# Adding the further spectral products of a block convolution by accumulating DMAs on GpSimd's queue instead of VectorE, with all orders searched anew

## The chip, the cores and the metric

The kernel runs on one core of a Trainium2 chip. The metric is device time in microseconds (us), from one launch. Times are medians over runs. The profile is one profiled execution, in microseconds from the first instruction.

## The reference

Two blocks, each used twice, on x of 2048 tokens by 512 channels in bfloat16. Block A is a long convolution with a gate; block B is a SwiGLU feed-forward network of width 1792. Cut to what matters:

```python
def A(n, k, v, shift_k, ssm_k, ssm_D):          # n = layernorm(x)
    k_shift = sum(k_pad[:, t:t + S, :] * shift_k[:, 3 - t] for t in range(4))
    kv = k_shift * v
    y = irfft(rfft(kv, 2 * S) * rfft(ssm_k, 2 * S))[:S]   # causal, length 2048
    return n * (y + kv * ssm_D)

def B(n, w_gate, w_up, w_down):
    return (silu(n @ w_gate) * (n @ w_up)) @ w_down

x = q
for _ in range(2):
    x = x + A(layernorm(x), k, v, shift_k, ssm_k, ssm_D)
    x = x + B(layernorm(x), w_gate, w_up, w_down)
```

The convolved sequence y does not depend on x: k, v and the filter are inputs. It is computed once and used by both layers.

## The kernel before

**Blocks and spectra.** The sequence is cut into four blocks of 512 tokens. The causal convolution of length 2048 becomes a convolution of blocks: a block k of the result is the sum of the products of the spectrum X[i] of an input block with the spectrum G[j] of a filter block over i + j = k. A spectrum is a tile of 128 partitions by 4096 bfloat16 elements, which is 1 MB: four residue classes, real and imaginary part, 512 channels.

**A product.** `product(i, j)` (L740) multiplies X[i] by G[j]. Two multiplications of 128x4096 (L765) write the temporaries t1 and t2. Two combinations of 128x2048 (L769) form the real and the imaginary part. For the first product that belongs to a Z[k] they write Z[k] itself. For a further product they write over t1, and an addition of 128x4096 (L773) adds t1 to Z[k]. All of these are on VectorE (DVE). Six products are further ones: (1,0) into Z[1]; (0,2) and (2,0) into Z[2]; (2,1), (0,3) and (3,0) into Z[3].

**From Z to the result.** `inverse(k)` (L786) folds a full Z[k] on DVE: two rows of 128x2048 into a tile m (L653), then two sums and differences (L659) and two rotated ones (L670) of 128x1024 each back into Z. TensorE (PE) multiplies the four residue classes with an inverse matrix (L423, `ps<-Z,inv`), and ScalarE (ACT) copies them into Yk. The `prologue` of a unit (a layer, a block and a half block of 256 tokens) multiplies Yk by the normalised x (L998), adds x (L999), and computes layer statistics (L926). A power on GpSimd (POOL, L912) makes rstd of them, which L976 uses on DVE to normalise z. Two transposing DMAs on SyncE's queue (SP, L1006) bring z into zT, which the gate and up matmuls of the unit read (L423, `pf<-wg_sb,zT` and others). The feed-forward part goes on with an activation and a copy on ACT (L1197, L1198), a product on DVE (L1201, L1204), transposing DMAs on SP (L1206) and down matmuls (L1287); L1258, L1262 and L1267 are the same for units whose rows need no transposing.

**The order.** Each operation is recorded with `add(engine, cost, ...)` into a `Plan`. A table ORDER of 1798 numbers, one for each operation in the order of recording, sorts them; each engine then issues its own operations strictly in that sequence. `Plan.walk` goes once through the sequence with the recorded costs to place buffers into slots (spectra, t1, t2 and others share a ring of 11 slots, "s8") and to place filler matmuls. POOL carries 32 powers of L912 after the setup and no DMA.

Of the kernel before, what the change touches and what calls it, by code (L numbers as in the profile page):

```python
# [14 lines left out]
ALU = mybir.AluOpType  # L15
# [7 lines left out]
K_ACT = lambda b: b in {2, 3}  # L23
PW = 0.7
# [326 lines left out]
def kernel(  # L351
# [14 lines left out]
    nc = tc.nc  # L366
# [46 lines left out]
    add = plan.add  # L413
# [326 lines left out]
    def product(i, j, slots=range(4), conv=True):  # L740
# [31 lines left out]
        if not first:  # L772
            dve(8 * D, lambda: nc.vector.tensor_add(out=z.t[:], in0=z.t[:], in1=t1.t[:]), [t1], [z], conv=conv)  # L773
# [832 lines left out]
```

## Time and profile before

| what | value |
|---|---|
| time, median of 3 runs | 338.73 us (338.35 to 338.96) |
| span of the profiled execution | 337.1 us |
| what lies around the span (median less span; the profiled execution's own whole time is not listed apart from its span) | 1.6 us |
| mean granted TensorE clock | 1.000 |
| additions of L773, six | 13.7 us on DVE |
| DMA data moved | 31.08 MB, of which 30.61 MB on SP's queue |

A row of the profile's groups gives line, engine, operation, tiles out and in, shape, count, then the busy time in us and the mean time of one in ns, then the idle time of the engine just before such rows. PE is the matmul stream and PEld the loading of weights beside it. A table by windows gives the busy time of each engine in a stretch. The chain of waits follows the last instruction back through what released each step.

### The profile page before, as it was taken

How to read it: one execution, taken by the hardware profiler on the slowest of the kernel's cores; microseconds unless marked ns; L12 is line 12 of the kernel's file. 1: busy time of each engine (PE TensorE's matmuls, PEld its weight loads, DVE VectorE, ACT ScalarE, POOL GpSimd, SP SyncE). 2: the span in 40 equal slices, each digit the busy share in tenths (PEclk: the TensorE clock that was granted, in tenths of full speed). 3: DMA queues.
4: the chain of work that ended last, by engine and by line, in shares of the span. 5: the costliest groups of instructions: out<-in, count | busy, mean ns of one | idle time of the engine just before them, and what ended most of it. 6: DMA issues, size and time to landing. Idle time of an engine off the chain costs nothing.

```text
span 337.1 us, 6249 instructions
## 1 busy us (share of the span) xinstructions
PE 332.4 (99%) x2300; PEld 208.0 (62%) x2300; DVE 314.3 (93%) x566; ACT 269.4 (80%) x550; POOL 36.1 (11%) x48
## 2 busy tenths in 40 slices
PE   9999999999999999999999999999999999999996
PEld 7665865645445564644545474654445787878994
DVE  7799999999999999999999999997898998986995
ACT  6999999999966684989999794989765748476862
POOL 4010100031210100022110200021000000000000
PEclk9999999999999999999999999999999999999999
DMA  7999403632354446253314433320415320203001
GB/s 278 331 281 387 65 3 77 140 93 34 78 94 86 95 88 146 72 80 74 69 33 83 104 81 102 81 53 10 84 33 95 65 65 16 42 8 64 2 33 62
DMA packets 75817, 31.08 MB, mean 92 GB/s; under 512 B 67589, under 2 KB 73610, under 8 KB 75786
## 3 DMA queue, kind: packets, MB, share of 16 engines
q1 hardware_dynamic: 75632, 30.61, 38.3%
q8 instruction: 18, 0.29, 0.4%
q14 instruction: 13, 0.11, 0.1%
q10 hardware_dynamic: 154, 0.07, 0.1%
HBM read 12.33 MB, written 2.10 MB: 43 GB/s over the span
## 4 chain that ended last, share of the span: by engine, by line
PE 85%; DVE 10%; ACT 2%; issue 1%; POOL 0%; POOLq 0%
PE pf L423 48%; PE pd L1287 19%; PE ps L1097 7%; PE ps L423 6%; PE pf L1171 4%; DVE t L755 1%; PE wm L1572 1%; DVE Z L759 1%; DVE bst L926 1%; DVE t L769 1%; ACT jk L950 1%; DVE Z L773 1%; DVE t L765 1%; DVE m L896 1%; DVE z L976 1%
## 5 line engine op out<-in xcount | busy, mean ns | idle before, releaser
L423 PEld LDWEIGHTS <-zT 128*128 128x128 bf16 x496 | 48.5, 98 | 55.1 <-issue 0.2
L423 PE MATMUL pf<-wu_sb,zT 128*128 128x512 bf16 x248 | 61.5, 379 | 0.0
L423 PE MATMUL pf<-wg_sb,zT 128*128 128x512 bf16 x248 | 61.4, 379 | 0.0
L423 PE MATMUL pf<-zT,wg_sb 128*128 128x256 bf16 x400 | 50.7, 273 | 0.3 <-DVE zT L1037 0.3
L1197 ACT ACTIVATE sg<-pf 128x512 bf16<-128x512 f32 x62 | 37.4, 615 | 14.9 <-PE pf L423 10.7
L1287 PE MATMUL pd<-wd_sb,sg 128*128 128x512 bf16 x200 | 48.9, 379 | 0.0
L1198 ACT CAST hr<-pf 128x512 bf16<-128x512 f32 x62 | 36.3, 599 | 12.7 <-PE pf L423 10.9
L423 PEld LDWEIGHTS <-wg_sb 128*128 128x128 bf16 x400 | 38.6, 98 | 8.3 <-issue 0.7
L765 DVE TENSOR_TENSOR t<-X,G 128x4096 bf16<-128x4096 bf16 x18 | 41.0, 2287 | 0.1
L1258 ACT ACTIVATE sg<-pf 128x512 bf16<-128x512 f32 x50 | 29.6, 603 | 7.7 <-PE pf L423 6.3
L423 PE MATMUL pf<-zT,wu_sb 128*128 128x256 bf16 x272 | 34.9, 273 | 0.1
L912 POOL TENSOR_TENSOR rstd<-mv,nhalf 128x2 f32<-128x2 f32 x20 | 18.3, 919 | 147.8 <-DVE mv L927 147.8
L1287 PEld LDWEIGHTS <-sg 128*128 128x128 bf16 x200 | 19.6, 98 | 21.4
L423 PEld LDWEIGHTS <-wu_sb 128*128 128x128 bf16 x272 | 26.5, 98 | 6.6 <-issue 0.4
L1287 PE MATMUL pd<-wd_sb,ht 128*128 128x512 bf16 (+1 forms) x126 | 29.6, 369 | 0.0
L912 POOL TENSOR_TENSOR rstd<-ve,nhalf 128x2 f32<-128x2 f32 x12 | 13.8, 1150 | 119.6 <-ACT ve L954 119.6
L926 DVE BATCH_NORM_STATS2 bst<-xc 128x6 f32<-128x512 bf16 x40 | 26.3, 685 | 0.3
L1262 ACT CAST ht<-pf 128x512 bf16<-128x512 f32 x34 | 20.2, 599 | 1.6 <-PE pf L423 1.5
L1287 PEld LDWEIGHTS <-ht 128*128 128x128 bf16 x126 | 12.3, 98 | 13.4 <-DVE ht L1267 0.4
L532 ACT ACTIVATE X<-ps 128x512 bf16<-128x512 f32 x32 | 18.6, 606 | 2.3 <-PE ps L423 1.6
L1267 DVE TENSOR_TENSOR ht<-ht,sg 128x1024 bf16<-128x1024 bf16 (+1 forms) x33 | 18.3, 556 | 0.7 <-ACT sg L1258 0.4
L1204 DVE TENSOR_TENSOR hr<-hr,sg 128x1024 bf16<-128x1024 bf16 x25 | 17.1, 683 | 1.3 <-ACT sg L1197 0.9
(157 smaller groups left out, 590.9 us busy)
## 6 DMA issues: line engine op xcount, KB each, us to landing
hn<-in_A_ssm_k_dram SPq DMA_DIRECT2D x4, 512.0 KB, 4.0
vt<-in_A_v_dram SPq DMA_DIRECT2D x4, 512.0 KB, 6.0
xc<-in_A_q_dram SPq DMA_DIRECT2D x4, 512.0 KB, 5.3
out_dram<-xc SPq DMA_DIRECT2D x15, 128.0 KB, 1.9
wg_sb<-in_B_w_gate_dram SPq DMA_DIRECT2D x1, 1792.0 KB
wu_sb<-in_B_w_up_dram SPq DMA_DIRECT2D x1, 1792.0 KB, 7.6
wd_sb<-in_B_w_down_dram SPq DMA_DIRECT2D x1, 1280.0 KB, 11.5
sg<-hr SPq DMA_TRANSPOSE x62, 2.4
```

Source lines behind the costliest of these rows:

```text
L423: nc.tensor.matmul(o, lhsT=lhsT, rhs=rhs, start=(n == 0), stop=(n == len(terms) - 1))
L532: add("ACT", act(D), lambda: nc.scalar.activation(out=view(), in_=ps.t[:], func=ACT.Copy, scale=scale), r=[ps], w=[(buf, keys)], conv=conv)
L765: dve(8 * D, lambda t=t, part=part: nc.vector.tensor_mul(out=t.t[:], in0=x.t[:, :, part:part + 1, :].to_broadcast((P, R, 2, D)), in1=g.t[: ...
L912: add("POOL", cost, lambda: nc.gpsimd.tensor_tensor(out=rstd.t[:], in0=var(), in1=nhalf.t[:].to_broadcast((P, n)), op=ALU.pow), r=reads + ...
L926: add("DVE", 0.6, lambda st=st, i=i: nc.vector.bn_stats(out=st.t[:, 0:6], in_=xs[c].t[:, i, :]), r=[(xs[c], (i,))], w=[st])
L1097: nc.tensor.matmul(bank.t[:, half_ * C:(half_ + 1) * C], lhsT=lhsT(i), rhs=rhs(i), start=(first and i == 0 and half_ == 0), stop=(last and ...
L1197: add("ACT", act(D), lambda ps=ps, dst=dst, o=o, which=which: nc.scalar.activation(out=rows(dst, o), in_=ps.t[:], func=ACT.Silu) if which ...
L1198: out=rows(dst, o), in_=ps.t[:], func=ACT.Silu) if which == "g" else nc.scalar.copy(out=rows(dst, o), in_=ps.t[:]),
L1258: add("ACT", act(D), lambda ps=ps, o=o, sg=sg: nc.scalar.activation(out=sg.t[:, o:o + 2, :], in_=ps.t[:], func=ACT.Silu), r=[ps], w=[(sg, ...
L1262: add("ACT", act(D), lambda ps=ps, o=o, ht=ht: nc.scalar.copy(out=ht.t[:, o:o + 2, :], in_=ps.t[:]), r=[ps], w=[(ht, (o // 2,))], due=(uni ...
L1267: dve(n * W, lambda sg=sg, ht=ht: nc.vector.tensor_mul(out=ht.t[:], in0=ht.t[:], in1=sg.t[:]), [sg], [ht], due=(unit, k / pairs, 0.0, "h"))
L1287: nc.tensor.matmul((pds[o] if not cs.start else pds[HP]).t[:, cs], lhsT=ht.tiles(q, o), rhs=wt["d"].t[:, ft, cs], start=(ft == std0 and no ...
```

## The change

`Z_DMA` is true for every pair. In place of the DVE addition of a further product, `product` records an accumulating DMA on GpSimd's queue: it reads t1 and the old Z, and writes their sum into Z, SBUF to SBUF. The table ORDER is replaced as a whole: each operation of the kernel may stand elsewhere.

```diff
@@ -21,6 +21,7 @@
 K_ACT = lambda b: b in {2, 3}
+Z_DMA = lambda i, j: True
 PW = 0.7
...
 ORDER = [
-    13, 127, 133, 202, 6, 0, 2, 4, 21, 5, 8, 1, 3, 9, 11, 17, 12, 18, 14, 19, 22, 20, 25, 24, 23, 26, 27, 37, 28, 31, 38, 69, 36, 60, 16, 52, 44,
...
+    10, 5, 7, 203, 0, 3, 4, 8, 17, 1, 2, 35, 37, 38, 89, 6, 12, 9, 11, 13, 22, 15, 18, 14, 16, 19, 20, 32, 33, 91, 95, 96, 39, 46, 49, 50,
...
@@ -769,7 +773,9 @@
-        if not first:
+        if not first and Z_DMA(i, j):
+            add("POOL", 1.3, lambda: nc.gpsimd.dma_start(out=z.t[:], in_=t1.t[:], accum_op=ALU.add, max_dma_last_dim=4096), r=[t1], w=[z], lat=7.0, conv=conv)
+        elif not first:
             dve(8 * D, lambda: nc.vector.tensor_add(out=z.t[:], in0=z.t[:], in1=t1.t[:]), [t1], [z], conv=conv)
```

The numbers 1.3 and 7.0 are what the planner counts for the DMA on POOL and until it has landed; they steer the order and the slots only. The operations of PE are the same in number (2267 matmuls and 33 fillers), in another order. The six DMAs are called A1 to A6 below, in the order of issue: A1 adds (1,0) to Z[1], A2 and A3 add (0,2) and (2,0) to Z[2], and A4 to A6 add (2,1), (0,3) and (3,0) to Z[3].

What stands where is shown at three places. A row is line, operation, tile written and tiles read (each with the number of its buffer), shape, and in brackets the semaphores it waits for: DVE_49 is VectorE's own, DMASW that of a GpSimd DMA, DMAHW that of a DMA of another queue. The lines of the changed kernel lie 4 to 6 further on: L653, L765, L769, L773, L912, L976, L1201 and L1267 of before are L657, L769, L773, L777 (now the DMA), L918, L982, L1207 and L1273.

VectorE before, around the last further product, (3,0) into Z[3]. The two rows z are the normalising for the unit of layer 2, block 2 (blocks count from 0), second half, whose transposed form zT PE waits for:

```order
L765 TENSOR_TENSOR t2_3060<-X3_2818,G0_255 128x4096 [waits DVE_49]
L1201 TENSOR_TENSOR hr_3062<-hr_3062,sg_3026 128x512 [waits Activation_49]
L976 TENSOR_SCALAR z_3069<-xc_1859,nm_3041,rstd_3067 128x512 [waits Pool_49]
L976 TENSOR_SCALAR z_3079<-xc_1859,nm_3041,rstd_3067 128x512 [waits DMAHW6_49]
L765 TENSOR_TENSOR t1_3081<-X3_2818,G0_255 128x4096
L769 TENSOR_TENSOR t1_3081<-t1_3081,t2_3060 128x4x512 [waits DVE_49]
L769 TENSOR_TENSOR t1_3081<-t1_3081,t2_3060 128x4x512
L1201 TENSOR_TENSOR hr_3062<-hr_3062,sg_3026 128x512 [waits Activation_49]
L773 TENSOR_TENSOR Z_2286<-Z_2286,t1_3081 128x4096 [waits DVE_49]
L653 TENSOR_TENSOR m_3098<-Z_2286 128x2048 [waits DVE_49]
```

VectorE in the changed kernel, at the same product:

```order
L769 TENSOR_TENSOR t1_3013<-X3_2734,G0_237 128x4096
L1210 TENSOR_TENSOR hr_2939<-hr_2939,sg_2997 128x1024 [waits Activation_49]
L773 TENSOR_TENSOR t1_3013<-t1_3013,t2_2962 128x4x512 [waits DVE_49]
L773 TENSOR_TENSOR t1_3013<-t1_3013,t2_2962 128x4x512
L982 TENSOR_SCALAR z_3101<-xc_1837,nm_3020,rstd_3099 128x512 [waits Pool_49]
L982 TENSOR_SCALAR z_3112<-xc_1837,nm_3020,rstd_3099 128x512 [waits DMAHW6_49]
L1207 TENSOR_TENSOR hr_3047<-hr_3047,sg_3029 128x512 [waits Activation_49]
L982 TENSOR_SCALAR n_3135<-xc_2648,mv_2732,rstd_2790 128x512
L1273 TENSOR_TENSOR ht_3069<-ht_3069,sg_3088 128x512 [waits Activation_49]
L982 TENSOR_SCALAR n_3135<-xc_2648,mv_2732,rstd_2790 128x512
L1207 TENSOR_TENSOR hr_3047<-hr_3047,sg_3029 128x512
L657 TENSOR_TENSOR m_3163<-Z_2264 128x2048 [waits DMASW5_49]
```

The second multiplication and the two combinations stood behind the rows z and stand ahead of them now; the addition is gone, and the first fold of Z[3] (m) waits for DMASW5, which is A6, with seven short rows between.

GpSimd before, at the same place (rstd_3067 is the one that the rows z read):

```order
L912 TENSOR_TENSOR rstd_2900<-ve_2898,nhalf_122 128x2 [waits Activation_49,Pool_49]
L912 TENSOR_TENSOR rstd_2969<-ve_2960,nhalf_122 128x2 [waits Activation_49]
L912 TENSOR_TENSOR rstd_3065<-mv_2766,nhalf_122 128x2 [waits DVE_49,Pool_49]
L912 TENSOR_TENSOR rstd_3067<-ve_3058,nhalf_122 128x2 [waits Activation_49,Pool_49]
L912 TENSOR_TENSOR rstd_3231<-mv_3218,nhalf_122 128x2 [waits DVE_49,Pool_49]
L912 TENSOR_TENSOR rstd_3388<-mv_3374,nhalf_122 128x2 [waits DVE_49,Pool_49]
```

GpSimd in the changed kernel (rstd_3099 is the one that the rows z read now):

```order
L918 TENSOR_TENSOR rstd_2827<-mv_2823,nhalf_87 128x2 [waits DVE_49,Pool_49]
L918 TENSOR_TENSOR rstd_2960<-ve_2958,nhalf_87 128x2 [waits Activation_49,Pool_49]
L918 TENSOR_TENSOR rstd_3099<-ve_3033,nhalf_87 128x2 [waits Activation_49,Pool_49]
L777 DMA Z_2264<-t1_3013 128x2x2048 [waits DMASW4_49,DVE_49]
L918 TENSOR_TENSOR rstd_3231<-mv_3228,nhalf_87 128x2 [waits DVE_49,Pool_49]
L918 TENSOR_TENSOR rstd_3440<-mv_3322,nhalf_87 128x2 [waits DVE_49,Pool_49]
```

A6 is queued right behind the power for the rows z, and the power of a later unit right behind A6.

VectorE before, at (0,2) into Z[2]; m and X2 are the folding of the input spectrum X[2], and t2_1792 belongs to the next product, (2,0):

```order
L769 TENSOR_TENSOR t1_1653<-t1_1653,t2_1650 128x4x512
L1267 TENSOR_TENSOR ht_1691<-ht_1691,sg_1738 128x1024 [waits DMAHW0_49,DMAHW5_49,PE_49,Activation_49]
L653 TENSOR_TENSOR m_1772<-X2_1492 128x2048 [waits DMAHW4_49,DMAHW3_49,DMAHW1_49]
L653 TENSOR_TENSOR m_1772<-X2_1492 128x2048
L659 TENSOR_TENSOR X2_1492<-m_1772 128x1024 [waits DVE_49]
L670 TENSOR_TENSOR X2_1492<-m_1772 128x2x512
L1267 TENSOR_TENSOR ht_1644<-ht_1644,sg_1779 128x512 [waits Activation_49]
L659 TENSOR_TENSOR X2_1492<-m_1772 128x1024
L670 TENSOR_TENSOR X2_1492<-m_1772 128x2x512
L765 TENSOR_TENSOR t2_1792<-X2_1492,G0_255 128x4096 [waits DVE_49]
L773 TENSOR_TENSOR Z_1614<-Z_1614,t1_1653 128x4096
```

VectorE in the changed kernel, at the same product:

```order
L773 TENSOR_TENSOR t1_1647<-t1_1647,t2_1642 128x4x512
L1345 TENSOR_TENSOR xc_301<-xc_301,dn_1684 128x1024 [waits Activation_49]
L657 TENSOR_TENSOR m_1733<-X2_1471 128x2048 [waits DVE_49]
L657 TENSOR_TENSOR m_1733<-X2_1471 128x2048
L674 TENSOR_TENSOR X2_1471<-m_1733 128x2x512 [waits DVE_49]
L1273 TENSOR_TENSOR ht_1703<-ht_1703,sg_1771 128x1024 [waits DMAHW6_49,DMAHW5_49,Activation_49]
L1273 TENSOR_TENSOR ht_1758<-ht_1758,sg_1769 128x512 [waits PE_49]
L663 TENSOR_TENSOR X2_1471<-m_1733 128x1024
L674 TENSOR_TENSOR X2_1471<-m_1733 128x2x512
L663 TENSOR_TENSOR X2_1471<-m_1733 128x1024
L769 TENSOR_TENSOR t1_1797<-X2_1471,G0_237 128x4096 [waits DVE_49]
L769 TENSOR_TENSOR t2_1799<-X2_1471,G0_237 128x4096 [waits DMASW1_49]
```

The addition at the end is gone. The second multiplication of the product (2,0) stands behind its first one, and waits for DMASW1, which is A2, since t2_1799 takes the slot that A2 reads from.

141 rows, old and new, of the table ORDER are left out of this document.

## Prediction

> **What bounds the kernel now.** I read the page's busy times first, then the windows, the waits of TensorE, the chain, and the timeline at the last product. The page, with busy time, share of the span and number of instructions:
>
> ```profile
> span 337.1 us, 6249 instructions
> PE 332.4 (99%) x2300; PEld 208.0 (62%) x2300; DVE 314.3 (93%) x566; ACT 269.4 (80%) x550; POOL 36.1 (11%) x48
> ```
>
> The span is 337.1 us and the median of the runs 338.73, so 1.6 us lie around the span. I take these 1.6 as unchanged: every term below is a difference in the span, and is put on 338.7. PE is busy 99% of it. The windows say where the rest is (length, then busy time of PE, PEld, DVE, ACT, POOL, the granted clock, the DMA share, GB/s):
>
> ```profile
> 0.00:33.00 33.00, 31.73 (x295) 21.76 (x295) 28.74 (x74) 29.03 (x59) 5.97 (x18) 1.00 1.00 319
> 33.00:60.00 27.00, 26.91 (x186) 18.23 (x187) 26.86 (x38) 26.86 (x60) 2.52 (x3) 1.00 0.32 54
> 160.00:210.00 50.00, 50.00 (x277) 26.94 (x276) 49.48 (x63) 41.66 (x80) 3.86 (x3) 1.00 0.35 79
> 235.00:262.00 27.00, 26.95 (x146) 13.86 (x145) 24.55 (x37) 18.16 (x37) 1.38 (x2) 1.00 0.36 69
> 300.00:334.00 34.00, 33.84 (x348) 29.32 (x346) 28.43 (x76) 23.08 (x47) 1.38 (x2) 1.00 0.13 29
> ```
>
> Ahead of 33 us PE idles 1.27 us (33.00 less 31.73), where no further product runs. In the three other windows with any idle time it is 0.09 + 0.05 + 0.16 = 0.30 us. DVE is nearly full (49.48 of 50), and PE does not wait for it. The waits of PE and its weight loads, largest of their kind (total, times, longest):
>
> ```profile
> PE ptz L1034 <- DVE z L976: 0.3, 1, 0.3
> PEld L1034 <- DVE z L976: 0.8, 1, 0.8
> PEld L423 <- DVE Z L659: 0.3, 1, 0.3
> PEld L423 <- DMA zT<-z: 0.2, 1, 0.2
> ```
>
> A weight load that waits costs PE only what its buffered matmuls do not cover, so these lines bound from above and the 0.30 us is the price. The bound is PE's own stream. A full DVE matters only where its work is just in time, and the chain goes over DVE at one of the six further products, (3,0) into Z[3] (start, length, step):
>
> ```profile
> 239.22 0.67 DVE z L976 x2
> 239.89 2.21 DVE t L765
> 242.12 2.36 DVE t L769 x2
> 244.82 2.21 DVE Z L773
> 248.62 1.15 DVE m L653
> 250.40 0.68 DVE Z L670
> ```
>
> **The change: what goes.** The groups concerned (count, then busy time and mean ns):
>
> ```profile
> L773 DVE TENSOR_TENSOR Z<-Z,t 128x4096 bf16<-128x4096 bf16 x6 | 13.7, 2287 | 0.0
> L765 DVE TENSOR_TENSOR t<-X,G 128x4096 bf16<-128x4096 bf16 x18 | 41.0, 2287 | 0.1
> L653 DVE TENSOR_TENSOR m<-Z 128x2048 bf16<-128x2048 bf16 x6 | 7.2, 1213 | 0.1
> L670 DVE TENSOR_TENSOR Z<-m 128x1024 bf16<-128x1024 bf16 x6 | 4.0, 680 | 0.0
> L976 DVE TENSOR_SCALAR z<-xc,nm,rstd 128x512 bf16<-128x512 bf16 x4 | 1.5, 408 | 0.0
> ```
>
> Six additions of 2.287 us leave DVE: 13.7 us of 314.3. Freed time on an engine for which PE hardly waits is worth at most PE's idle time, 0.30 us after 33 us. I take -0.3, with ends 0 and -0.3. The start has the same instructions in another order: 0, with ends of -1.27 (all idle time gone) and +1.3 (the same again).
>
> **What comes: the price of one accumulating DMA.** No row shows one. The nearest are plain loads (KB, median us to landing), and POOL's powers, which share the engine that issues it (min/median/max ns):
>
> ```profile
> hn<-in_A_ssm_k_dram SPq DMA_DIRECT2D x4, 512.0 KB, 4.0
> wu_sb<-in_B_w_up_dram SPq DMA_DIRECT2D x1, 1792.0 KB, 7.6
> L912 POOL TENSOR_TENSOR rstd<-mv,nhalf x20: 688/812/1503, 30.4 to 306.7; 128x2 f32<-128x2 f32 x20
> L912 POOL TENSOR_TENSOR rstd<-ve,nhalf x12: 687/750/2863, 17.2 to 238.4; 128x2 f32<-128x2 f32 x12
> ```
>
> From 512 to 1792 KB it is 3.6 us for 1.25 MB, 2.9 us a MB. One MB moved plainly comes to 4.0 + 1.4 = 5.4 us; counting the two MB that an addition reads, 8.3. I take the middle, 6.9, since reading and writing may overlap. POOL's share I bound by its shortest and longest power, 0.7 and 2.9, and take 1.1, near the medians. From issue to landing that makes 8.0 us, with ends of 6.1 and 11.2. POOL is 11% busy; behind a DMA in its queue stands a power at most, which a POOL held for 2.9 us would delay by that much.
>
> **Where the landing is waited for.** The order of the changed kernel gives the rows between the end of a product and the first row that needs its DMA. For A2 they are two folds (2.4), four rotations and sums (2.7), three rows xc and ht (1.8: two of L670's size, one of L976's) and a multiplication (2.3): 9.2 us. A1, A3 and A4 have 9 to 11 us by the same count, and A5 far more. At 8.0 none of these waits; at 11.2 A2 waits 2.0 and the others up to 2.2, each after a saving of 2.3 in the same queue. Behind the waiting t2 in A2's case are only DVE's products, which PE reads much later. I take 0 for A1 to A5.
>
> A6 has seven rows of about 0.41 us, 2.9 us, before the first fold of Z[3], so DVE will wait there with everything behind it: the fold, the products hr of the feed-forward part, then the prologue of block 3. What counts is when PE is late. The timeline of before there (start, length, engine, line; in brackets the idle time before it):
>
> ```profile
> 238.43 0.69 POOL L912 TENSOR_TENSOR rstd<-ve,nhalf 128x2 f32<-128x2 f32 x1 [6.19 <-ACT ve L954]
> 239.15 0.73 DVE L976 TENSOR_SCALAR z<-xc,nm,rstd 128x512 bf16<-128x512 bf16 x2
> 239.59 2.52 SPq L1006 DMA_TRANSPOSE zT<-z  x2
> 242.26 1.03 PE L423 MATMUL pf<-wg_sb,zT 128*128 128x512 bf16 x4
> 243.12 1.03 PE L423 MATMUL pf<-wu_sb,zT 128*128 128x512 bf16 x4
> 251.32 1.03 PE L423 MATMUL ps<-Z,inv 128*128 128x512 bf16 x4
> ```
>
> In the changed kernel the product ends ahead of the rows z, and A6 stands behind the same power in POOL, so it is issued at 239.1 (238.43 + 0.69). PE needs Z[3] two matmuls earlier than before, at 251.32 - 0.43 = 250.9 (four matmuls take 0.86 us, from 242.26 to 243.12). Two folds and one sum ahead of that are 2.4 + 0.7 = 3.1 us, and the hand-over 0.3 by the wait on L659 above. So A6 must land by 247.5, 8.4 us after its issue. At 8.0 it does, and the wait costs nothing; at 11.2 it is 2.8 us late, at 6.1 2.3 early. I take 0, with ends 0 and 2.8.
>
> By the Trainium skill, page "SBUF — State Buffer", section "Who interferes with whom", a DMA issued by GpSimd can starve for the writing of its descriptors while DVE runs an instruction in a two-port mode, which tensor_scalar can enter and a product of two tensors cannot. By that rule A6 would wait for the two rows z, landing about 0.7 later and 0.3 late, and the sum below would be 0.3 higher; the spread of POOL's powers, 0.69 to 2.86 us, shows that something holds POOL, though not that it holds descriptors.
>
> **What runs beside it.** The landings in the view of the tile zT in this stretch; the queue of SP at 61 us, where a load stands ahead of transposes, with these transposes' landings; and the landings of all transposes of that line:
>
> ```profile
> DMA to landing us min/median/max: 2.4/2.4/2.4
> ```
>
> ```profile
> 61.65 0.58 SPq L495 DMA_DIRECT2D vt<-in_A_v_dram  x1
> 63.56 2.52 SPq L1206 DMA_TRANSPOSE sg<-hr  x2
> ```
>
> ```profile
> DMA to landing us min/median/max: 2.6/3.0/3.3
> DMA to landing us min/median/max: 2.3/2.4/4.3
> ```
>
> ```profile
> sg<-hr SPq DMA_TRANSPOSE x62, 2.4
> zT<-z SPq DMA_TRANSPOSE x30, 2.4
> ```
>
> The first transpose, issued at 239.59, lands at 242.0, and PE uses it at 242.26 in before: no slack. In the changed kernel PE's first matmul on this zT has the same place in its stream, and the two transposes run while A6 moves its data. Behind a load transposes took 0.2 to 0.9 longer than the median 2.4, and of the 62 of sg<-hr none more than 1.9. I take +1.0, the middle of 0.2 and 1.9, with ends of 0 (the DMA share in this window is only 0.36) and 5.1 (the transposes land with A6, at 247.1 instead of 242.0). The other accumulates keep the queues busy for 5 x 8 us in which about a dozen transposes of the 92 (62 and 30) run; their cover in the new order is mostly several us, as it is for most of before, whose PE loads waited 0.2 on a zT. I take one more such delay of the middle size halved, +0.5, ends 0 and 1.9.
>
> **The sum:** 338.7 - 0.3 + 0 + 0 + 1.0 + 0.5 = 339.9 us.
>
> **The rivals.** *Hidden (R1).* The transposes are issued half a microsecond after A6 and could be done before POOL has the bulk of its data on the way; A6 lands in time; PE stays at 99%. For it: the DMA share of 0.36 and PE's 50.00 us of 50 in the window from 160, although DVE is full there. Against: the zT with no slack. 338.4 to 339.2, middle 338.7.
>
> *Faster (R2).* With 13.7 us off DVE the rows that fed PE just in time come early, the new order closes the start as well, and no transpose is late. This decides if A6 lands by 247.5 and zT by 242.3. At best all idle time goes: 338.7 - 0.30 - 1.27 = 337.2; with half of the start's, 337.8. Against: nothing in the change touches the start but its order, and the chain's DVE steps there cost PE almost nothing.
>
> *Slower by the queue (R3).* Transposes consist of small packets:
>
> ```profile
> DMA packets 75817, 31.08 MB, mean 92 GB/s; under 512 B 67589, under 2 KB 73610, under 8 KB 75786
> ```
>
> Nearly all of 67589 packets under 512 B belong to about a hundred transposes, over 600 each, or 40 on each of 16 DMA engines. A6 has 256 rows of 4 KB, 16 on each. If the engines take the queues in turn, packet by packet, a transpose is not through before A6 is, and zT lands with it: +5.1, and 338.7 - 0.3 + 5.1 + 0.5 = 344.0. For it: transposes behind a load were late. Against: that was one queue, and no row shows two busy queues. The Trainium skill, page "DMA: Bandwidth & Descriptors", section "Queues, rings and completion order", says that each DMA engine goes round its queues by whole packets, which is this rival's rule; no run here shows it.
>
> **How the numbers follow.** About 0.2%, 0.7 us, is what a measurement of this kernel can tell from no change. The forecast has 0.45, with a range of its own of 339.1 to 341.7 (the zT term from 0.2 to 1.9, A6 up to 0.9 late). R1 has 0.28, R2 0.15 and R3 0.12. Faster (under 338.0): R2 and 0.02 of R1, 0.17. Same (338.0 to 339.4): the rest of R1 and 0.03 of the forecast, 0.29. Slower: 0.54. The range leaves out the lower half of R2 and R3's middle and above: 337.4 to 343.0.
>
> **What would show it.** Right: L777 lands 6 to 11 us after its issue; DVE idles at m<-Z behind A6 by about 5 us (8.0 less 2.9) and PE there by under 1; zT<-z beside A6 takes 3 to 4.3 us and PE waits for it; DVE busy is near 300 us. Wrong: no PE wait on zT and none at Z[3] (R1); PE idle ahead of 33 us clearly under 1.27 (R2); zT landing only with A6 (R3); a landing over 11 us, with DVE waiting at A1 to A4 too and PE waiting behind, would break the price itself.

## The result, and the profile after

The changed kernel takes 368.4 us (median of 4 runs, 364.9 to 368.6), the kernel before 338.5. The ratio is 1.086, with a 95% interval of 1.081 to 1.090. The forecast was 339.9 with a range up to 343.0. It named the side rightly and had 1.2 us for what became 29.9.

The page of the changed kernel, with the clock that was granted to TensorE in forty slices:

```profile
span 366.8 us, 6221 instructions
PE 339.5 (93%) x2270; PEld 209.6 (57%) x2300; DVE 304.6 (83%) x560; ACT 271.3 (74%) x550; POOL 40.8 (11%) x54
PEclk9999999999999969969999899999969999999999
```

DVE is busy 9.7 us less, near the 300 foreseen. PE fell from 99% to 93% of a span that is 29.7 us longer, and its clock, 1.00 throughout before, dips in four places. What PE waited for, and what DVE waited for at the landings:

```profile
PE pd L1293 <- DMA sg<-hr: 12.6, 3, 5.2
PE pf L427 <- DMA zT<-z: 6.9, 2, 6.8
PE ps L427 <- DVE Z L663: 0.8, 1, 0.8
```

```profile
DVE m L657 <- DMA Z<-t: 7.9, 2, 6.7
```

TensorE waits 19.5 us for transposes (12.6 and 6.9), where before a weight load waited 0.2 for one at most. The landing of the accumulating DMAs themselves is waited for by DVE alone (7.9 us here and 0.4 at a product). Their price, and the longest landing of the transposes sg<-hr:

```profile
Z<-t POOLq DMA_DIRECT2D x6, 1024.0 KB, 9.3
```

```profile
DMA to landing us min/median/max: 8.5/9.3/11.5
DMA to landing us min/median/max: 2.3/2.5/8.5
```

The first of the two lines is that of L777, 8.5 to 11.5 us; the second that of L1212 (L1206 before), of which the slowest took 4.3 before. The place of A6, in the order of the timeline that the prediction showed of before (POOL, SP, PE):

```profile
259.89 1.22 POOL L777 DMA_DIRECT2D Z<-t  x1
260.41 4.23 SPq L1012 DMA_TRANSPOSE zT<-z  x2
269.59 1.89 PE L427 MATMUL pf<-wu_sb,zT 128*128 128x512 bf16 x4 [6.79 <-DMA zT<-z]
271.27 1.91 PE L427 MATMUL pf<-wg_sb,zT 128*128 128x512 bf16 x4
275.64 1.03 PE L427 MATMUL pf<-wg_sb,zT 128*128 128x512 bf16 x4
276.50 1.03 PE L427 MATMUL pf<-wu_sb,zT 128*128 128x512 bf16 x4
```

```profile
DMA to landing us min/median/max: 8.3/8.7/9.1
```

Both transposes of zT land after 8 to 9 us in place of 2.4, together with A6 (issued at 259.9, landed 9.6 later), and PE stands for 6.79 us. Behind the stall a group of four matmuls takes 1.68 us (269.59 to 271.27) in place of 0.86 (275.64 to 276.50): half speed. Stalls stand beside A2 (5.19 us), A3 (4.34) and A4 (3.11) too, with transposes sg<-hr:

```profile
134.16 1.89 PE L1293 MATMUL pd<-wd_sb,sg 128*128 128x512 bf16 x4 [5.19 <-DMA sg<-hr]
157.61 4.82 PE L1293 MATMUL pd<-wd_sb,sg 128*128 128x512 bf16 x11 [4.34 <-DMA sg<-hr]
206.15 4.02 PE L1293 MATMUL pd<-wd_sb,sg 128*128 128x512 bf16 x10 [3.11 <-DMA sg<-hr]
```

Why the transposes land late can be seen piece by piece, as the trace records each packet of the 16 DMA engines. Counted by microsecond of start, beside A6 and beside A4:

```text
us      256-byte pieces of transposes   4-KB pieces   mean of a 4-KB piece
263     46                              48 of A6      0.33 us
264     45                              45 of A6      0.34 us
265     47                              46 of A6      0.33 us
266     44                              48 of A6      0.34 us
269     877                             none
199     0                               47 of A4      0.39 us
200     0                               47 of A4      0.36 us
201     0                               47 of A4      0.38 us
```

Beside A6 the pieces of the two queues alternate one for one: some 45 pieces of transposes in a microsecond, against 877 in the one without A6. A transpose of 128 KB has 512 pieces, 32 for each engine, and A6 has 16 for each. Of the first zT 131 pieces passed before A6's first one, which came 1.9 us after the issue. The others took turns until 267.6, it landed at 269.5 as A6 did, and the second zT passed its first piece only at 267.6. Beside A2 it is the same, with 178 and 175 pieces in the 4 us from 128.2. Beside A4 there were no turns: of the transposes issued at 198.1 and 200.2 the first piece passed at 203.0, when nine tenths of A4's pieces had started. Beside A3 the second transpose waited likewise, from 148.7 to 154.1. What lets a transpose take turns in one place and not in the other is not shown. In both cases it ends as the rival R3 said: a transpose is not through before the large DMA nearly is.

By the Trainium skill, page "DMA: Bandwidth & Descriptors", section "Queues, rings and completion order", an engine goes round its queues packet by packet, with typically 9 to 17 descriptors (orders for one piece) in a packet. The trace agrees in kind beside A2 and A6, with one descriptor as the packet, and shows no such round beside A4.

The trace also records the granted clock as stretches: 0.5 for 6.83, 6.83, 3.41 and 6.83 us, each around the end of one of the four stalls or right behind it, and 1.0 between. The matmuls that ran in them, for 4.2, 4.6, 3.4 and 5.3 us behind the stalls, took twice their time, which is half of it lost: 8.7 us in all.

So the 29.7 us are made up as follows: 5.2 + 4.3 + 3.1 + 6.8 = 19.4 us of stalls at A2, A3, A4 and A6; 8.7 us at half speed behind them; 0.8 us at A1, where PE waits for the fold of Z[1]; and 0.6 us at the start, where PE waits for a load. That is 29.5; some 0.2 us is spread over the rest.

### The profile page after: what moved, and what is told of

Read it like the earlier page. It is cut to its first block, busy times and chain, and to the rows that moved or that the text cites. A ratio compares the mean times of both kernels' runs of the same rounds, so it can differ in the third digit from the quotient of the medians.

```text
span 366.8 us, 6221 instructions
## 1 busy us (share of the span) xinstructions
PE 339.5 (93%) x2270; PEld 209.6 (57%) x2300; DVE 304.6 (83%) x560; ACT 271.3 (74%) x550; POOL 40.8 (11%) x54
## 4 chain that ended last, share of the span: by engine, by line
PE 68%; DMA 15%; DVE 9%; ACT 4%; issue 2%; SPq 1%; POOL 1%; DVEq 0%; POOLq 0%
PE pf L427 38%; PE pd L1293 15%; DMA sg<-hr 7%; PE ps L1103 6%; PE ps L427 5%; PE pf L1177 3%; DMA zT<-z 3%; DMA Z<-t 3%; DMA kn<-in_A_k_dram 1%; DVE t L759 1%; ACT sg L1203 1%; DVE m L657 1%; DVE t L773 1%; DVE Z L763 1%; DVE bst L932 1%
## 5 line engine op out<-in xcount | busy, mean ns | idle before, releaser
L427 PE MATMUL pf<-wu_sb,zT 128*128 128x512 bf16 x244 | 62.8, 388 | 7.0 <-DMA zT<-z 6.8
L1293 PE MATMUL pd<-wd_sb,sg 128*128 128x512 bf16 x193 | 53.0, 414 | 13.0 <-DMA sg<-hr 12.6
L427 PE MATMUL pf<-zT,wg_sb 128*128 128x256 bf16 x400 | 49.5, 273 | 0.5 <-DVE zT L1043 0.5
L1293 PEld LDWEIGHTS <-sg 128*128 128x128 bf16 x200 | 20.4, 104 | 39.0 <-DMA sg<-hr 14.4
L1203 ACT ACTIVATE sg<-pf 128x512 bf16<-128x512 f32 x62 | 36.4, 603 | 8.2 <-PE pf L427 4.7
L769 DVE TENSOR_TENSOR t<-X,G 128x4096 bf16<-128x4096 bf16 x18 | 41.2, 2288 | 0.5 <-DMA Z<-t 0.4
L1264 ACT ACTIVATE sg<-pf 128x512 bf16<-128x512 f32 x50 | 29.7, 603 | 13.8 <-PE pf L427 9.5
L918 POOL TENSOR_TENSOR rstd<-mv,nhalf 128x2 f32<-128x2 f32 x20 | 19.4, 972 | 133.8 <-DVE mv L933 133.8
L1293 PE MATMUL pd<-wd_sb,ht 128*128 128x512 bf16 (+1 forms) x123 | 28.7, 370 | 0.2
L1273 DVE TENSOR_TENSOR ht<-ht,sg 128x1024 bf16<-128x1024 bf16 (+1 forms) x33 | 18.2, 557 | 5.5 <-ACT sg L1264 4.5
L918 POOL TENSOR_TENSOR rstd<-ve,nhalf 128x2 f32<-128x2 f32 x12 | 10.7, 891 | 100.8 <-ACT ve L960 100.8
L1341 ACT ACTIVATE dn<-pd 128x512 bf16<-128x512 f32 x10 | 6.0, 617 | 19.5 <-PE pd L1293 19.5
```

What stands on the lines that cost most here:

```text
L427: nc.tensor.matmul(o, lhsT=lhsT, rhs=rhs, start=(n == 0), stop=(n == len(terms) - 1))
L769: dve(8 * D, lambda t=t, part=part: nc.vector.tensor_mul(out=t.t[:], in0=x.t[:, :, part:part + 1, :].to_broadcast((P, R, 2, D)), in1=g.t[: ...
L918: add("POOL", cost, lambda: nc.gpsimd.tensor_tensor(out=rstd.t[:], in0=var(), in1=nhalf.t[:].to_broadcast((P, n)), op=ALU.pow), r=reads + ...
L1203: add("ACT", act(D), lambda ps=ps, dst=dst, o=o, which=which: nc.scalar.activation(out=rows(dst, o), in_=ps.t[:], func=ACT.Silu) if which ...
L1264: add("ACT", act(D), lambda ps=ps, o=o, sg=sg: nc.scalar.activation(out=sg.t[:, o:o + 2, :], in_=ps.t[:], func=ACT.Silu), r=[ps], w=[(sg, ...
L1273: dve(n * W, lambda sg=sg, ht=ht: nc.vector.tensor_mul(out=ht.t[:], in0=ht.t[:], in1=sg.t[:]), [sg], [ht], due=(unit, k / pairs, 0.0, "h"))
```

## The experiments

These theories stood against each other. Q: the accumulating DMAs and the transposes take turns on the DMA engines, and late transposes stall PE. O: the new order is slow by itself. P: each such DMA costs a fixed 5 us. V: DVE's waits for the landings are what costs. F, later: GpSimd's queue itself, not its bytes. All kernels start from the changed one unless said otherwise. The kernel before took 338.3 to 338.5 us beside them.

**The additions back on VectorE, in the new order.**

```diff
-Z_DMA = lambda i, j: True
+Z_DMA = lambda i, j: False
```

> The new order with all six additions back on VectorE, at the places where the DMAs were issued. Theory Q (the accumulating DMAs and the transposes share the 16 DMA engines in turns, transposes land late, TensorE stalls): no stall of TensorE over 1 us, clock back at 1.00, 338 to 343 us. Rival O (the new order itself is what is slow): 355 us or more.

347.5 us, 1.027 of before (1.024 to 1.030). Neither theory had that: 21 us of the 30 go with the DMAs, but 9 stay. Its PE waits are many and short, the longest 2.0 us and so over Q's 1; the two largest:

```profile
PE pd L1293 <- DMA sg<-hr: 3.1, 2, 2.0
PE ps L427 <- DVE vt L733: 1.1, 2, 0.8
```

Whether the order or the 13.7 us of additions, for which this order has no place, costs the 9 us was left to a cleaner run (the small DMAs below).

**A6 alone by DMA.**

```diff
-Z_DMA = lambda i, j: True
+Z_DMA = lambda i, j: (i, j) in {(3, 0)}
```

> The new order, only A6 (3,0) by DMA, the other five on VectorE. Theory Q: zT beside A6 lands after 8 us or more and TensorE waits about 7 us for it; with a lower clock behind the stall the time is that of the order alone plus 7 to 10 us. Rival O: the time of the order alone, within 1 us. Rival P (each accumulating DMA costs about 5 us whatever lies beside it): plus 5.

353.7 us, 6.2 more than the order alone; PE waits 4.1 us for zT. O falls. The size is below Q's 7 to 10 and does not exclude P's 5. The packets say why it is below. A6's first piece came 2.4 us after its issue in place of 1.9, so 405 of the first zT's 512 pieces were ahead of it (131 in the changed kernel), and this zT landed after 6.4 us in place of 9.1. What a transpose pays beside a large DMA thus hung on half a microsecond here; why the first piece came later is not shown. The run with A6 in full among small DMAs asks again on clean ground.

**A1 and A5 alone by DMA.**

```diff
-Z_DMA = lambda i, j: True
+Z_DMA = lambda i, j: (i, j) in {(1, 0), (0, 3)}
```

> The new order, only A1 (1,0) and A5 (0,3) by DMA, the two beside which few or no transposes were issued. Theory Q: within 1.5 us of the order alone. Rival P (each accumulating DMA costs about 5 us): plus 10. Rival V (VectorE's waits for the landing are what costs): within 1 us, as these two were not waited for.

345.4 us, 2.1 less than the order alone: P falls, 12 us away. That two DMAs make it faster is more than Q or V said. The two additions that leave DVE may be the reason, since the small DMAs below show that additions on DVE are what costs in this order.

**Small pieces.**

```diff
-accum_op=ALU.add, max_dma_last_dim=4096
+accum_op=ALU.add, max_dma_last_dim=1024
```

> All six by DMA as in the changed kernel, but cut into pieces of 1 KB in place of 4 KB (same bytes). Theory Q: a 256-byte piece of a transpose then waits for about a quarter as long at each turn, so transposes beside an accumulating DMA land after 5 to 7 us in place of 8 to 9, each stall is 2 to 3 us shorter, and the time falls to 355 to 364 us, unless the small pieces make the DMA itself much longer. Rivals O and V: 366 us or more.

362.9 us, 5.5 less than the changed kernel, within Q's range, though the DMA itself became longer (median landing 10.6 us for 9.3). A piece of 1 KB took 0.115 us in place of 0.36. The stalls bear Q's reason out in part only. At A2 and A6 they fell, from 5.2 to 2.9 and from 6.8 to 3.7 us; at A3 and A4 they grew, from 4.3 to 4.7 and from 3.1 to 4.2. The transposes of zT beside A6:

```profile
DMA to landing us min/median/max: 4.7/7.0/9.3
```

The first was quick because all of its 512 pieces passed before A6's first one, which came 2.5 us after its issue. The second passed its first piece 4.2 us after its issue and then took turns, some 142 pieces of each queue in a microsecond. So a turn is shorter with small pieces, but at A6 the gain came as much from the later start. O would have given no change. V falls: DVE's waits for the landings grew from 8.3 to 12.3 us, and the time fell.

**Plain copies.** This leaves out the addition to the old Z.

```diff
-nc.gpsimd.dma_start(out=z.t[:], in_=t1.t[:], accum_op=ALU.add, max_dma_last_dim=4096)
+nc.gpsimd.dma_start(out=z.t[:], in_=t1.t[:], max_dma_last_dim=4096)
```

> The changed kernel with its six DMAs as plain copies of t1 over Z (same bytes written, 4 KB pieces, same queue); leaves out the addition to the old Z. Theory Q, with a piece of the accumulating DMA at 0.35 us on each DMA engine because two operands are read: a plain 4 KB piece takes about half, the DMA is through in 5 to 6 us, transposes beside it land after 4.5 to 6 us, and the time is 348 to 357 us. Rival F (the queue of GpSimd itself, not the bytes, holds the transposes): as the changed kernel, 365 to 369.

348.4 us, at the lower end of Q's range. The landing took 5.5 us and a 4-KB piece about 0.18; zT beside it landed after 4.6 to 5.6, and PE stood for 3.3. F falls: with the same queue and the same number of pieces the stalls shrink with the time of a piece. A piece that accumulates thus takes twice as long as one that copies. There were no turns here: the first zT, issued at 244.5, passed its first piece at 248.0, when 99% of the copy's pieces had started.

**Small DMAs.** Each accumulates 64 of 4096 elements of a row; most of the sum is left out.

```diff
+FULL = lambda i, j: False
...
+            piece = (lambda t: t[:]) if FULL(i, j) else (lambda t: t[:, 0, 0, 0:64])
-            add("POOL", 1.3, lambda: nc.gpsimd.dma_start(out=z.t[:], in_=t1.t[:], accum_op=ALU.add, ...
+            add("POOL", 1.3, lambda: nc.gpsimd.dma_start(out=piece(z.t), in_=piece(t1.t), accum_op=ALU.add, ...
```

> The changed kernel with each accumulating DMA cut down to 64 of 4096 elements of a row (16 KB in place of 1 MB), so that order, queue, waits and issue stay and the bytes go; leaves out the rest of the sum. Theory Q: no stall, clock 1.00, 337.5 to 341 us; then the order by itself is about as good as the one before, and all of the 30 us are the bytes beside the transposes. Rival O (the new order is slow by itself, as the run with all additions on VectorE could mean): 345 us or more. Rival F: 355 or more.

338.9 us, 1.001 of before (1.000 to 1.002). O falls for good: the order, the queue and the six issues, with the additions off DVE, come to 0.4 us, and the bytes cost the other 29.5. Its page and DMAs:

```profile
span 336.6 us, 6221 instructions
PE 330.0 (98%) x2270; PEld 208.0 (62%) x2300; DVE 303.7 (90%) x560; ACT 270.9 (80%) x550; POOL 39.3 (12%) x54
PEclk9999999999999999999999999999999999999999
```

```profile
Z<-t POOLq DMA_DIRECT2D x6, 16.0 KB, 2.4
```

DVE is as free of the additions as in the changed kernel, and the time is that of before: with additions that cost nothing, this order would have brought nothing. The 9 us of the first experiment are then the additions on DVE in an order made without them.

**Small DMAs, but A6 in full.** The edit is against the run with six small ones, here and in the next three. Most of the other five sums is left out.

```diff
+FULL = lambda i, j: (i, j) == (3, 0)
```

> As the run with small DMAs, but A6 with its full 1 MB; leaves out most of the other five sums. Theory Q: zT beside A6 lands after about 8 us, TensorE waits 5 to 7 us, the clock behind it is lowered; 6 to 9 us more than with six small ones. The forecast of the prediction would be 1 to 2 more.

347.5 us, 8.6 more than with six small ones; Q's 6 to 9. This is the price of A6 alone, which the prediction had as 1.0. The windows at the stall (PE busy 3.38 of 10 us, DMA share 0.97) and behind it:

```profile
240.00:250.00 10.00, 3.38 (x16) 1.38 (x15) 2.88 (x7) 0.90 (x2) 0.49 (x1) 0.85 0.97 157
250.00:262.00 12.00, 11.95 (x47) 5.13 (x47) 5.15 (x8) 5.96 (x11) 0.00 (x0) 0.84 0.02 5
262.00:275.00 13.00, 12.78 (x99) 8.13 (x98) 11.73 (x32) 8.23 (x17) 1.42 (x2) 1.00 0.38 80
```

PE waits 6.6 us for zT, and the clock behind is 0.84 in a window with a DMA share of 0.02.

**Small DMAs, but A1 and A5 in full.** Most of the other four sums is left out.

```diff
+FULL = lambda i, j: (i, j) in {(1, 0), (0, 3)}
```

> As the run with small DMAs, but A1 and A5 with their full 1 MB; leaves out most of the other four sums. Theory Q: few transposes beside them, none waited for at once; 0 to 2 us more than with six small ones. Rival P (each full DMA costs the same): 10 more.

339.8 us, 0.9 more: a full DMA beside which no transpose is urgent costs next to nothing. P falls again.

**Small DMAs, but A2 to A4 in full.** Most of the other three sums is left out.

```diff
+FULL = lambda i, j: (i, j) in {(0, 2), (2, 0), (2, 1)}
```

> As the run with six small DMAs, but A2, A3 and A4 with their full 1 MB; leaves out most of the other three sums. Theory Q, if the four stalls of the changed kernel (5.2, 4.3 and 3.1 us beside A2 to A4, 6.8 beside A6) are each set by the DMA beside them: three stalls of that size, each with a lowered clock behind it, 338.9 + 12.6 + about 7 = 357 to 360 us. If the stalls feed one another, clearly less.

356.4 us, 17.5 more, half a microsecond below the expected range; PE waits 11.8 us for sg<-hr. The parts add up: 8.6 + 0.9 + 17.5 = 27.0 of the 29.5 us between the small DMAs and the full ones.

**A stall without a large DMA.** Small DMAs, with the first multiplication of (3,0) done four times; most of six sums is left out.

```diff
...
+                for _ in range(4 if (i, j, part) == (3, 0, 0) else 1)][-1], ...
```

> As the run with six small DMAs, with the first multiplication of (3,0) done four times, so that the rows z come 6.9 us later and TensorE stalls there with no large DMA beside it; leaves out most of six sums. Theory C (the lowered clock behind a stall comes from TensorE's idling): half speed behind the stall as with the full A6, 346 to 349 us. Rival (it comes from the DMA traffic): clock 1.00, 343.5 to 345.5 us.

346.3 us, 7.4 more. The place behind the stall:

```profile
246.03 3.59 PE L1296 MATMUL pd<-wd_sb,sg 128*128 128x512 bf16 x8 [5.58 <-DMA sg<-hr]
249.42 1.91 PE L428 MATMUL pf<-wu_sb,zT 128*128 128x512 bf16 x4
254.16 1.03 PE L428 MATMUL pf<-wg_sb,zT 128*128 128x512 bf16 x4
```

Here the DMAs land late because DVE is late, and the half speed is there again, for 6.83 us of granted clock 0.5. It comes with PE's stall, then, and needs no large DMA.

By the Trainium skill, page "TensorE: Matmul & The Clock Gate", section "Part 1: The HAM clock gate", half clock follows an idle window of about 3.4 us and lasts until a busy one, on a clock that runs freely. The stretches of 3.41 and 6.83 us, one such window and two, agree. That a whole window must be idle does not agree: half clock followed stalls of 2.0 us (the first experiment), 2.4 (small pieces), 3.1 (A4 in the changed kernel) and 3.3 us (plain copies). It did not follow stalls of 2.0 us in the third experiment, 2.6 among the plain copies and 2.9 among the small pieces. So in these runs every stall of 3.1 us or more was followed by half clock, and one of 2.0 to 2.9 us was in some executions only. Four executions of the first experiment's kernel had mean granted clocks of 0.994, 0.998, 0.995 and 1.000, at 348.6, 346.6, 348.4 and 346.5 us.

**The kernel before, with (0,3) alone by DMA.** Its own order, its DVE addition replaced at the same place.

```diff
-        if not first:
+        if not first and (i, j) == (0, 3):
+            add("POOL", 1.3, lambda: nc.gpsimd.dma_start(out=z.t[:], in_=t1.t[:], accum_op=ALU.add, max_dma_last_dim=4096), ...
+        elif not first:
```

> The kernel before with its own order, only (0,3) by DMA at the place where VectorE added it. Theory Q: VectorE's 2.3 us are worth nothing, and transposes sg<-hr issued 6.5 us behind the DMA, which are just in time there, come late: 338.5 to 342 us. The gain that the rival R2 of the prediction hoped for would show as 338.0 us or less.

343.1 us, 1.013 of before (1.011 to 1.015): slower, and more so than expected. The transposes hit were not the ones named. Their queue, and their landings in the kernel before and here:

```profile
207.41 8.68 SPq L725 DMA_TRANSPOSE kc<-ka  x4
```

```profile
DMA to landing us min/median/max: 2.3/2.4/2.4
DMA to landing us min/median/max: 2.8/7.9/8.6
```

The waits that came of it:

```profile
PE ps L423 <- DVE vt L729: 3.1, 2, 2.1
DVE vt L729 <- DMA kc<-ka: 4.6, 1, 4.6
```

Of the four transposes kc<-ka the first is issued 0.9 us after the DMA. They land up to 8.6 us after their issue, DVE waits 4.6 us for them, and PE 3.1 us for DVE; 3.41 us of half clock follow. A queue that is held up for 9 us reached PE here through the transposes that happened to be next.

## Why the prediction was wrong, point by point

- **The bound and what goes: right.** PE's own stream bounds this kernel, and 10 to 14 us off DVE are worth nothing. The small DMAs show it for this order: +0.4 us where -0.3 was taken, with PE at 98%.
- **The start: about right.** In the run with small DMAs PE idles 1.7 us ahead of 33 us for 1.27 before, and the span as a whole is 0.5 shorter. In the changed kernel PE waits 0.6 there for a load; all this lies within the ends.
- **The price of one accumulating DMA: mis-sized by little.** 8.0 us taken, with ends of 6.1 and 11.2; measured 8.5 to 11.5, median 9.3. The sum from rows of plain loads took reading and writing as half overlapped; a 4-KB piece that accumulates took 0.36 us (A6) and a plain one 0.18, so the second operand costs its full time. The weighed rule that A6's descriptors might wait 0.7 us for the two rows z did not show: its first piece started 1.9 us after the issue, those of A4 and A5 1.9 and 1.8.
- **No wait at A1 to A5: nearly right.** A1, beside a load of 512 KB, landed after 11.5 us, past the upper end; DVE waited 1.2 us for it and PE 0.8 behind that. At A2 DVE waited 0.4.
- **The wait for A6 at Z[3]: right, but covered.** DVE waited 6.7 us (5 foreseen), and PE did not wait for Z[3], since zT held it already.
- **"I take +1.0" for zT beside A6: the step that failed first.** It measured 6.6 to 6.8 us. The 0.2 to 1.9 came from transposes behind a load in their own queue; two busy queues are another case, and the prediction had said that no row shows it. The DMA share of 0.36, cited for a small cost, is a mean over 27 us; while A6 ran it was 0.91 (262 to 272 us). R3 had the right outcome at A6, 5.1 us, with a chance of 0.12. Its turns are what the trace shows there (32 pieces of a transpose for each engine, where R3 counted 40), and not what it shows beside A4. Its 344.0 was still 24 us short, as it took A6 alone and left the clock out.
- **"+0.5" for the other accumulates: the step that failed by more.** 12.6 us of stalls stand beside A2, A3 and A4. R3's rule was applied to A6 alone. That "their cover in the new order is mostly several us" was no help: several microseconds do not cover a landing of 7 to 9, and the transposes queued behind each DMA were never laid beside the order.
- **The clock: missing from the sum.** 8.7 us at half speed behind four stalls. No row of before could price it, as its clock was 1.00 in every window, but a stall of several microseconds was in the rivals without it.
- **Slower: right, for R3's reason and not for the forecast's.** The likeliest case was taken as a small version of the true one.

## What to carry to other kernels

Before work is moved from an engine to a DMA, list for each new transfer which small transfers are issued within its landing time and who waits for them: in the changed kernel the transposes that PE waited for landed within about 1.2 us of the large DMA, whether their pieces took turns or they got none. Relief for an engine that the bounding engine does not wait for is worth nothing; here a run with the added work all but left out told that at once. A stall of TensorE of 3 to 7 us cost its length and then 1.7 to 2.6 us more at half clock.

## What the runs showed of the hardware that was not expected

- An accumulating SBUF-to-SBUF DMA of 1 MB landed after 9.3 us, a plain copy of the same bytes after 5.5, and one of 16 KB after 2.4. Pieces of 4 KB took 0.36 us on a DMA engine when accumulating and 0.18 when copying; an accumulating piece of 1 KB took 0.115 (all beside zT).
- Beside A2 and A6 pieces of GpSimd's queue and of SyncE's alternated one for one, 4 KB against 256 bytes: some 45 pieces of each in a microsecond, where transposes without A6 passed 877. Beside A4 a transpose passed its first piece 4.9 us after its issue; the first zT beside A6 did after 1.2.
- How many of a transpose's 512 pieces passed before the large DMA's first piece went with its landing: 131, 164, 405 and 512 pieces with 9.1, 8.9, 6.4 and 4.7 us (the first zT in the changed kernel, with A6 in full among small DMAs, with A6 alone by DMA, and with small pieces).
- TensorE at half clock came in stretches of 3.41 or 6.83 us around the end of a stall or right behind it, with and without a large DMA, after stalls as short as 2.0 us.
